# Block-sparse attention and SwiGLU: chunk 0's feed-forward part in float16, with the weights' low parts made on GpSimd

## The chip, the cores and the metric

The kernel runs on one core of one Trainium2 chip. The metric is the device time of one execution in microseconds (us), as the median of several runs. A core has five engines, each with an instruction queue of its own that it works through in order: TensorE (PE in the profile; its weight loads are PEld), VectorE (DVE), ScalarE (ACT), GpSimd (POOL) and SyncE (SP), which here only starts transfers. An instruction that waits for a semaphore holds up everything behind it on its engine.

## The reference

Four batches of eight heads attend over 768 positions of 64 numbers each. The mask lets a block of 32 rows see its neighbours, the first and the last block, and three sampled ones; the first and the last block see everything. The result, as x with 512 columns, goes through a SwiGLU feed-forward part with 1536 inner columns:

```python
scores = scale * np.matmul(q, k.transpose(0, 1, 3, 2))
scores = np.where(mask, scores, -1000000000.0)
attn = np.exp(scores - np.max(scores, axis=-1, keepdims=True))
attn = attn / (np.sum(attn, axis=-1, keepdims=True) + 1e-09)
attn_out = np.matmul(attn, v)
x = np.ascontiguousarray(attn_out.transpose(0, 2, 1, 3)).reshape(B * S, H * D)
g = x @ w_gate
silu = g * (1.0 / (1.0 + np.exp(-g)))
return (silu * (x @ w_val)) @ w_out
```

All inputs arrive as float64, seen by the kernel as pairs of int32.

## The kernel before, in words

The 3072 rows of x are worked on in eight **chunks**, two to a batch, of 384 rows each. A chunk first has its attention: query blocks (32 rows, 8 heads) in pairs, and in odd chunks the two blocks that see everything (`full_rows`). Names carry the block's number: `qk_13` are scores, `pv_13` products with the values, `p_5` a gate or value product of the feed-forward part, `po_0` an output product.

**Precision.** Nearly all matmuls take float16 operands in two parts: a high part (the rounded number) and a low part (what is left of it). Three products, high by high, high by low and low by high, are summed. Operands are first scaled by a power of two that comes from a norm: squares with their sum on ACT (`square_w`), a matmul with ones on PE (`norm`, `col_sums`), four small integer operations on DVE (`pow2`). `split_w` then makes the high part of a weight tile of 128x512 on ACT (`hi_part`, line 354) and the low part on DVE (`lo_part`, line 357). Both overwrite the float32 tile that stands one place ahead in the same memory, so tile f can be split only after tile f−1.

**Weights.** There are 36 such tiles: gate and value (w1raw, in memory `w_99` and `w_100`), and output (w2raw, in `w_101`), 12 of each. Each is loaded by one transfer and decoded from float64 to float32 by three DVE operations (`to_f32`, lines 382 to 384).

**Feed-forward part of a chunk** (`ffn`). For each of 12 inner tiles f: gate product and value product on PE (12 matmuls each, line 1369), tanh on ACT, two multiplications on DVE, the high part of h on ACT (1387) and its low part on POOL (1390). Then three output products `po_t` of 36 matmuls, each evacuated by ACT (1305). Chunk 0 is the exception: `ffn_first` multiplies the float32 x, which `x_keep` put aside, with the float32 weights (lines 1255 and 1291), so it needs neither norms nor splits. The weights' norms and splits come later, with ranks 14 and 16, during and after this part and before chunk 1's.

**Chunk 0's attention** also differs (`first`): the probabilities are turned by matmuls with a diagonal matrix that carries the softmax's reciprocals (`dg`, DVE line 1106; `turn_pe`; `turned_high` on ACT; `turned_low` on DVE, line 1128), not by transfers. Its keys are gathered into `kring` by POOL (lines 1002 to 1005), in later chunks by DVE. The values of every pair of blocks are gathered by a transfer that POOL starts (`vring`, line 1016).

**Order.** Nothing runs in the order of the source. Every piece of work is a task of a `Plan` with an engine, a duration in us, a rank and the buffers it takes from rings. `Plan.order` runs through time: whenever an engine is free, it takes the ready task of lowest rank whose buffers are free. The rank is moved by the table `SHIFT`, keyed by the piece of work. The durations therefore decide the order of each engine's queue, but at run time only semaphores hold it. `DMA_US` and `SEM_US` are the plan's times for a transfer's landing and a semaphore.

## Time and profile before

| Quantity | us |
|---|---|
| median of three runs | 847.31 |
| the three runs | 847.08, 849.96, 847.31 |
| profiled execution, its own time | 845.61 |
| its span in the profile | 843.8 |

The profile covers one execution. Its span is 1.8 us shorter than that execution's time, and that execution is 1.7 us below the median. The granted TensorE clock was 0.965 of full speed on average. Busy times overlap, so they don't add up to the span. A line of a group reads: line of the program, engine, operation, output<-inputs, shapes, count | busy us, mean ns of one | idle time of the engine ahead of it, and what ended that idle time. A line of the chain reads: start, duration, what. A line of an engine's timeline begins with start and duration too, and has in brackets how long the engine had been idle and what it waited for. A line of the windows has the stretch, its length and the busy us of PE, PEld, DVE, ACT and POOL with the number of instructions, then the granted clock, the share of transfers and GB/s.

### The profile page before, as it was taken

To read this page: it belongs to the slowest core of one execution; us is meant where nothing else is said; L and a number is where in the kernel's file an instruction comes from. 1 tells how busy PE (TensorE), PEld (TensorE's weight loads), DVE (VectorE), ACT (ScalarE), POOL (GpSimd) and SP (SyncE) were. 2 spreads that over 40 slices of the span, in tenths; PEclk is the share of its full clock that TensorE was granted. 3 is DMA by queue.
4 is the path that set the end of the run, shared out by engine and by line. 5 is a ranking of instruction groups with operands and counts; after the bars stand their busy time and mean duration, and the time that the engine had idled before them with its cause. 6 is when DMAs were issued, how large, how long until landed. Compare 5 with 4: busy or idle time off the path is not lost.

```text
span 843.8 us, 20625 instructions
## 1 busy us (share of the span) xinstructions
PE 769.2 (91%) x7634; PEld 460.9 (55%) x7634; DVE 592.1 (70%) x1784; ACT 528.4 (63%) x1266; POOL 200.7 (24%) x258
## 2 busy tenths in 40 slices
PE   0267799979999999999999999998999999999997
PEld 0246655545465655665566556663566556655653
DVE  5987989858888976896488757852679769821320
ACT  5855845669786766788467757873458658821220
POOL 5574100002014321231223211321123212310220
PEclk9757999989999999999999999999999999999999
DMA  9999785789947897899878876988847964820001
GB/s 292 256 280 274 213 241 164 146 200 185 220 128 220 186 228 138 191 180 232 218 179 180 182 167 132 199 173 243 210 96 143 193 145 103 169 57 26 1 1 38
DMA packets 196309, 144.05 MB, mean 171 GB/s; under 512 B 133104, under 2 KB 156272, under 8 KB 196208
## 3 DMA queue, kind: packets, MB, share of 16 engines
q1 hardware_dynamic: 190576, 125.42, 65.2%
q0 software_dynamic: 5632, 17.31, 8.3%
q8 instruction: 60, 0.98, 0.5%
q14 instruction: 41, 0.34, 0.1%
HBM read 86.58 MB, written 12.58 MB: 118 GB/s over the span
## 4 chain that ended last, share of the span: by engine, by line
PE 68%; DMA 15%; DVE 7%; ACT 3%; issue 3%; SPq 2%; POOL 1%; DVEq 0%; ACTq 0%; POOLq 0%
PE p L1369 33%; PE po L1416 13%; DMA pts<-pp 6%; PE pv L1168 6%; PE p L1255 5%; PE po L1291 4%; PE qk L1030 3%; DMA w<-vd 2%; DVE w L383 2%; DVE w L384 1%; PE pvf L875 1%; DMA qn<-in_q_dram 1%; DMA kraw<-in_k_dram 1%; PE qkf L806 1%; DMA qs<-qraw 1%
## 5 line engine op out<-in xcount | busy, mean ns | idle before, releaser
L1369 PE MATMUL p<-xt,w 128*128 128x384 f16 x2016 | 340.3, 326 | 0.0
L1369 PEld LDWEIGHTS <-w 128*128 128x128 f16 x2016 | 191.9, 98 | 128.4 <-issue 6.2
L1416 PE MATMUL po<-w,h 128*128 128x512 f16 x756 | 171.1, 381 | 0.0
L1390 POOL TENSOR_TENSOR h<-act,h 128x384 f16<-128x384 f32 x84 | 80.0, 953 | 304.4 <-ACT h L1387 304.1
L1016 POOL DMA_INDIRECT vring<-vd,vidx x82 | 78.6, 959 | 280.4 <-PE pv L1168 236.9
L1416 PEld LDWEIGHTS <-h 128*128 128x128 f16 x756 | 71.9, 98 | 87.2 <-issue 7.1
L1376 DVE SCALAR_TENSOR_TENSOR act<-act,p 128x384 f32<-128x384 f32 x84 | 46.1, 549 | 64.3 <-ACT act L1373 62.6
L1168 PEld LDWEIGHTS <-vring 128*128 128x128 f16 x1968 | 68.9, 99 | 28.2 <-issue 16.2
L357 DVE SCALAR_TENSOR_TENSOR pp<-e,rr,pp 128x256 f16<-128x256 f32 x152 | 77.7, 552 | 7.5 <-ACT pp L354 6.2
L1168 PE MATMUL pv<-pts,vring 128*128 128x64 f16 x1968 | 72.3, 194 | 11.0 <-DMA pts<-pp 6.3
L1373 ACT ACTIVATE act<-p,gsc 128x384 f32<-128x384 f32 x84 | 48.4, 577 | 52.8 <-PE p L1369 45.2
L1095 ACT ACTIVATE e<-e,nb,es 128x256 f32<-128x256 f32 x132 | 78.2, 593 | 2.2
L1387 ACT CAST h<-act 128x384 f16<-128x384 f32 x84 | 42.5, 505 | 54.4 <-DVE act L1379 53.9
L354 ACT ACTIVATE pp<-e,rr 128x256 f16<-128x256 f32 x152 | 67.8, 497 | 10.3 <-DMA ptsf<-ppf 3.6
L1255 PE MATMUL p<-xt,w 128*128 128x384 f32 x192 | 70.1, 520 | 1.3 <-ACT xt L1134 1.0
L1379 DVE SCALAR_TENSOR_TENSOR act<-act,hs,p 128x384 f32<-128x384 f32 x84 | 51.3, 611 | 22.9 <-PE p L1369 21.7
L1255 PEld LDWEIGHTS p<-xt,w 128*128 128x128 f32 x192 | 37.6, 202 | 27.6 <-issue 5.3
L1076 DVE CUSTOM_DVE_ANT_1 e<-qk,msk 128x256 f32<-128x256 f32 x132 | 50.0, 416 | 0.5 <-PE qk L1030 0.3
L1005 DVE COPY kring<-kst 128x256 f16 x228 | 46.0, 258 | 4.9 <-PE pv L1168 1.6
L1305 ACT ACTIVATE ot<-po,oc 128x512 f32<-128x512 f32 x21 | 14.4, 686 | 52.7 <-PE po L1416 52.2
L1194 DVE TENSOR_TENSOR xt<-pv,xt 64x256 f16<-64x256 f32 x76 | 31.9, 420 | 17.2 <-ACT xt L1189 14.1
L361 ACT ACTIVATE wsq<-w 128x512 bf16<-128x512 f32 x36 | 22.6, 628 | 25.6 <-DVE w L384 16.4
(168 smaller groups left out, 983.0 us busy)
## 6 DMA issues: line engine op xcount, KB each, us to landing
vring<-vd SPq DMA_DIRECT2D x82, 192.0 KB
w1raw<-in_w_dram SPq DMA_DIRECT2D x24, 512.0 KB
qs<-qraw SPq DMA_DIRECT2D x84, 128.0 KB
qn<-in_q_dram SPq DMA_DIRECT2D x48, 128.0 KB
w2raw<-in_w_dram SPq DMA_DIRECT2D x12, 512.0 KB
vfull<-vd SPq DMA_DIRECT2D x12, 512.0 KB
qraw<-in_q_dram SPq DMA_DIRECT2D x42, 128.0 KB
out_dram<-ot SPq DMA_DIRECT2D x20, 256.0 KB
```

The lines of the kernel that those rows point to most:

```text
L354: nc.scalar.activation(hi, src, AF.Copy, scale=scale)
L357: nc.vector.scalar_tensor_tensor(lo, src, scale, hi, op0=ALU.mult, op1=ALU.subtract)
L1016: nc.gpsimd.indirect_dma_start(vf[0:96, 1, :], None, bt.vd, bass.IndirectOffsetOnAxis(ap=vidx[0:96, qb : qb + 1], axis=0))
L1076: nc.vector.tensor_tensor_reduce(ev[:, g], stv[:, g], o.g.msk[:, qb, :].unsqueeze(2).broadcast_to([P, 8, BLK]), scale=1.0, scalar=-3.0e38, ...
L1095: nc.scalar.activation(ev[:, g], sv[:, g], AF.Exp, bias=nb_[:, g : g + 1], scale=o.g.es[:, 0:1], accum_out=c["rs"][:, g : g + 1],)
L1168: nc.tensor.matmul(pvv[:, j, n % 2], vg[:, cc, l, 2 * j : 2 * j + 2, :], pq[:, g, m, cc, u : u + 2, :], start=i == 0, stop=i == 5,)
L1255: nc.tensor.matmul(buf.tile[:, 0:T], wst[m][:, f + 1, k_ * P : (k_ + 1) * P], x_f32()[:, k_, :], start=k_ == 0, stop=k_ == NKT - 1,)
L1369: nc.tensor.matmul(t[:, 0:T], w_[:, f, m, k_, :], xt.tile[:, l, k_, :], start=i == 0, stop=i == 11)
L1373: nc.scalar.activation(get(act, f"act_{ci}_{f}"), pg.tile[:, 0:T], AF.Tanh, scale=c["gsc"][:, f : f + 1])
L1379: nc.vector.scalar_tensor_tensor(act.tile, act.tile, c["hs"][:, 1:2], pw.tile[:, 0:T], op0=ALU.mult, op1=ALU.mult)
L1390: nc.gpsimd.tensor_tensor(hv()[:, 1, :], act.tile, hv()[:, 0, :], op=ALU.subtract)
L1416: nc.tensor.matmul(po.tile, hv[:, l, ts_], wo16[:, f, m, :], start=f == 0 and i == 0, stop=f == NF - 1 and i == 2)
```

## The change

Chunk 0's feed-forward part now runs through `ffn(0)`, like the others': `ffn_first`, `x_keep` and `x_f32` are gone. The first-layer weights are scaled in three groups of inner tiles (0 and 1, 2 to 5, 6 to 11); a group's norm takes all its squares and those before it. `split_w` has three steps on two engines: POOL scales the float32 tile in place, ACT casts it to the high part, POOL subtracts that to get the low part. The diagonals of chunk 0 are made by ACT. The two edge key blocks of chunk 0 are copied by one DVE operation, not by two of POOL. All durations of the plan, the ranks of the splits and the whole of `SHIFT` are new.

```diff
-W1_DEC, W2_DEC, W1_SPLIT, W2_SPLIT = 3.0, 5.0, 14.0, 16.0
+W1_DEC, W2_DEC, W1_SPLIT, W2_SPLIT = 3.0, 5.0, 3.05, 5.5
+W1_GROUPS = ((0, 2), (2, 6), (6, 12))
-DMA_US = 2.0
-SEM_US = 0.1
+DMA_US = 2.2
+SEM_US = 0.16
 SHIFT = {
-    "a0.0": -105.32, "a0.1": 0.02, "a0.2": -38.31, "a1.0": -72.7, "a1.1": -11.99, "a1.2": -2.34, "a2.0": -13.58, "a2.1":
+    "a0.0": -202.11, "a0.1": 56.45, "a0.2": -35.15, "a1.0": -198.18, "a1.1": -93.69, "a1.2": -28.19, "a2.0": -10.14,
...
-    t_rep = add("POOL", 8.0, repeats, [t_tab], rank=TAB)
+    t_rep = add("POOL", 17.0, repeats, [t_tab], rank=TAB)
...
     def split_w(m, f, scale, rank, need, last):
         src, hi, lo = wst[m][:, f + 1, :], w16[m][:, f, 0, :], w16[m][:, f, 1, :]
-        before = w_read[m][f - 1] if f else []
-        t1 = add("ACT", 0.72, lambda: hi_part(hi, src, scale), need + before + [last], rank)
-        return add("DVE", 0.75, lambda: lo_part(lo, src, scale, hi), [t1], rank)
+        before = v_first[RING] if m == 2 and f == 0 else []
+        t0 = add("POOL", 0.85, lambda: nc.gpsimd.tensor_scalar(src, src, scale, None, op0=ALU.mult), need, rank)
+        t1 = add("ACT", 0.6, lambda: nc.scalar.copy(hi, src), before + [t0, last], rank)
+        return add("POOL", 1.2, lambda: nc.gpsimd.tensor_tensor(lo, src, hi, op=ALU.subtract), [t1], rank)
...
     def split_w1(rank):
         last = [None, None]
-        for f2 in range(0, NF, 2):
+        for f0, f1 in W1_GROUPS:
+            fs, k = slice(f0, f1), f1 - f0
...
+            t = add("PE", 0.08, norm, sq + [x[0] for x in w1_split[-1:]], rank + 0.1 * f0, take=[n])
+            t = add("DVE", 0.75, scale, [t], EVAC, use=[n])
...
+        def edges():
+            two = bt.ks.tile.rearrange("p h (s k) -> p h s k", k=BLK)
+            nc.vector.tensor_copy(kg[:, :, 3:8:4, :], two[:, :, 0 : NB : NB - 1, :])
...
-            if first:
-                d = get(dg, f"dg_{nq}").bitcast(F32).rearrange("p (g q) -> p g q", g=4)
-                for g in range(2):
-                    nc.vector.tensor_scalar(d[:, g], ident, c["rr"][:, g : g + 1], None, op0=ALU.mult)
+        def diagonal():
+            d = get(dg, f"dg_{nq}").bitcast(F32).rearrange("p (g q) -> p g q", g=4)
+            for g in range(2):
+                nc.scalar.activation(d[:, g], ident, AF.Copy, scale=c["rr"][:, g : g + 1])
...
+        gated = {}
+        for f0, f1 in W1_GROUPS if ci == 0 else ((0, NF),):
+            t = add("DVE", 0.15, lambda fs=slice(f0, f1): gate_scale(fs), [w1_split[f1 - 1][0], batches[b].vsc_t], EVAC)
...
     decode_w1(W1_DEC)
+    split_w1(W1_SPLIT)
     decode_w2(W2_DEC)
-    ffn_first(1000.0)
+    split_w2(W2_SPLIT)
+    ffn(0, 1000.0)
...
-        if ci == 1:
-            split_w1(W1_SPLIT)
-            split_w2(W2_SPLIT)
```

Three places of the queues show what the new order does. The first is **PE** in the middle of chunk 0's gate and value products (`p_5` and its neighbours; `nrm_w` is the norm of a group of weights). Before:

```order
L1255 MATMUL p_5_2006<-xt_124,w_99 128x384 x4
L1255 MATMUL p_5_2022<-xt_124,w_100 128x384 x4
L1255 MATMUL p_6_2040<-xt_124,w_99 128x384 x4
L1255 MATMUL p_6_2061<-xt_124,w_100 128x384 x2
L351 LDWEIGHTS ones_h
L351 MATMUL nrm_w_2_2068<-wacc,ones_h 128x4
L1255 MATMUL p_6_2061<-xt_124,w_100 128x384 x2
```

and now:

```order
L1314 LDWEIGHTS w_99
L1314 MATMUL p_5_2136<-xt_125,w_99 128x384
L355 LDWEIGHTS ones_h
L355 MATMUL nrm_w_6_2159<-wacc,ones_h 128x12
L1314 LDWEIGHTS w_100
L1314 MATMUL p_5_2161<-xt_125,w_100 128x384
```

The last group's norm, which needs the squares of all tiles 6 to 11, stands between the gate and the value product of tile 5; before, a norm of two tiles stood there and no product needed it.

The second is **POOL** behind the last key copies and gathers of chunk 0. Before, it has only gathers of values and then the low parts of chunk 1's h:

```order
L1016 DMA vring_113<-vd_115,vidx 96x1024
L1016 DMA vring_114<-vd_115,vidx 96x1024
L1016 DMA vring_112<-vd_115,vidx 96x1024
L1390 TENSOR_TENSOR h_0_3539<-act_0_3517,h_0_3539 128x384
L1390 TENSOR_TENSOR h_0_3539<-act_1_3567,h_0_3539 128x384
L1390 TENSOR_TENSOR h_2_3715<-act_2_3660,h_2_3715 128x384
```

and now, where the last group's scale has come (w0 and w1 are the gate and value tiles):

```order
L1335 TENSOR_TENSOR h_0_4_2157<-act_0_4_2112,h_0_4_2157 128x384
L422 TENSOR_SCALAR w0_99<-w0_99,wsc_102 128x512
L422 TENSOR_SCALAR w1_100<-w1_100,wsc_102 128x512
L422 TENSOR_SCALAR w0_99<-w0_99,wsc_102 128x512
L422 TENSOR_SCALAR w1_100<-w1_100,wsc_102 128x512
L1335 TENSOR_TENSOR h_0_4_2157<-act_0_5_2174,h_0_4_2157 128x384
L422 TENSOR_SCALAR w0_99<-w0_99,wsc_102 128x512
L422 TENSOR_SCALAR w1_100<-w1_100,wsc_102 128x512
L422 TENSOR_SCALAR w0_99<-w0_99,wsc_102 128x512
L424 TENSOR_TENSOR w0_99<-w0_99 128x512
L424 TENSOR_TENSOR w1_100<-w1_100 128x512
```

Seven scalings and one low part of h now stand ahead of the first subtraction of the last group, which ends the split of tile 6.

The third is **DVE** at the last first-layer weight that it decodes (w1raw_6_1, tile 6's value weights), now:

```order
L1321 SCALAR_TENSOR_TENSOR act_0_4_2112<-act_0_4_2112,p_0_4_2088 128x384
L386 TENSOR_SCALAR w1_100<-w1raw_6_1_2049 128x512
L387 SCALAR_TENSOR_TENSOR w1_100<-w1raw_6_1_2049,w1_100 128x512
L388 SCALAR_TENSOR_TENSOR w1_100<-w1raw_6_1_2049,w1_100 128x512
L1324 SCALAR_TENSOR_TENSOR act_0_4_2112<-act_0_4_2112,hs_0_1967,p_0_4_2114 128x384
L386 TENSOR_SCALAR w2_101<-w2raw_3_2076 128x512
L387 SCALAR_TENSOR_TENSOR w2_101<-w2raw_3_2076,w2_101 128x512
L388 SCALAR_TENSOR_TENSOR w2_101<-w2raw_3_2076,w2_101 128x512
L346 TENSOR_SCALAR p2_w1_6_2177<-nrm_w1_6_2159 128x12
```

One more output weight is decoded between that weight and the powers of two of the last group; the split of tiles 6 to 11 waits for these.

244 lines of the change are left out of this document (92 added, 152 removed), and 97 rows, old and new, of the table SHIFT.

## The prediction, made before the result was known

> **What bounds the kernel now.** I read the busy shares and the chain of waits first, then the stretch around chunk 0's feed-forward part.
>
> ```profile
> PE 769.2 (91%) x7634; PEld 460.9 (55%) x7634; DVE 592.1 (70%) x1784; ACT 528.4 (63%) x1266; POOL 200.7 (24%) x258
> PE 68%; DMA 15%; DVE 7%; ACT 3%; issue 3%; SPq 2%; POOL 1%; DVEq 0%; ACTq 0%; POOLq 0%
> ```
>
> TensorE (PE) is busy for 91% of the span and carries 68% of the chain. Where are the other 9%? The windows give busy time of PE, weight loads, DVE, ACT and POOL in each stretch (then granted clock and DMA share).
>
> ```profile
> 84.00:105.00 21.00, 15.46 (x295) 13.04 (x294) 19.83 (x48) 17.00 (x45) 4.09 (x4) 0.92 0.76 212
> 105.00:126.00 21.00, 21.00 (x66) 11.83 (x65) 17.45 (x35) 9.64 (x25) 0.00 (x0) 0.92 0.84 244
> 168.00:189.00 21.00, 14.91 (x187) 9.13 (x188) 11.78 (x40) 12.04 (x35) 1.83 (x2) 0.84 0.83 190
> 231.00:843.00 612.00, 599.93 (x5828) 353.55 (x5826) 400.67 (x1287) 374.74 (x896) 142.32 (x150) 1.00 0.70 151
> ```
>
> From 231 us on PE idles 12 us in 612. So the change's worth is settled by when chunk 1's feed-forward part starts; I call that point T1. All of chunk 1's attention stands ahead of T1 on PE in both orders, so what T1 moves, the end moves. POOL does nothing at all from 105 to 126 us.
>
> The chain shows each kind of matmul alone, then PE's own rows the two ends and the waits:
>
> ```profile
> 102.46 10.93 PE p L1255 x24
> 155.06 4.07 PE p L1255 x12
> 189.59 1.29 PE p L1255 x4
> 203.26 5.25 PE po L1291 x12
> 769.48 46.80 PE p L1369 x288
> 816.28 23.32 PE po L1416 x108
> ```
> ```profile
> 172.07 0.27 PE L1051 MATMUL qk<-kst,qs 128*32 128x96 f16 x8 [3.29 <-ACT e L1095]
> 183.79 0.91 PE L1168 MATMUL pv<-pts,vring 128*128 128x64 f16 x14 [2.60 <-DMA pts<-pp]
> 221.78 0.81 PE L1337 MATMUL xn<-sqx,ones_h 128*128 128x384 bf16 x4
> 231.12 6.01 PE L1369 MATMUL p<-xt,w 128*128 128x384 f16 x36
> ```
>
> T1 is 231.1 before. Chunk 0's gate and value products run from 102.5 to 190.9 (88.4 us), its output products from there to T1 (40.2 us).
>
> **What the matmuls give.** Float32 gate and value: 192 records of 4.07/12 = 0.339 us, 65.1 us; a whole float16 chunk is 46.8. That is 18.3 less. Output: 72 of 5.25/12 = 0.4375 us, 31.5, against 23.3: 8.2 less. Chunk 0 now needs the x norm too, four matmuls, some 0.7. So 25.8 us less on PE. Of the 88.4 us, 65.1 are those matmuls at full clock, 2.7 more the slow clock of the first 24 (10.93 against 24 × 0.339 = 8.2), some 6 the two idle times shown; the remaining 14.5 are chunk 1's attention, the same list in both orders. PE alone would need 46.8 + 14.5 + 0.7 = 62 us from p_0 to the end of p_11, then 40.2 − 8.2 = 32 to T1. By PE alone T1 would be 102.5 + 62 + 32 = 196.5, 35 earlier. But float32 products need no scaled weights; the float16 ones do, and that work now stands ahead of them.
>
> **What now comes first.** The split costs, per weight tile of 128x512, one POOL scaling, one ACT cast and one POOL subtraction; 36 tiles. On POOL only these rows come near:
>
> ```profile
> L1390 POOL TENSOR_TENSOR h<-act,h 128x384 f16<-128x384 f32 x84 | 80.0, 953 | 304.4 <-ACT h L1387 304.1
> L329 POOL TENSOR_SCALAR dup<-dup 128x192 f32<-128x192 f32 x1 | 0.7, 695 | 0.1
> L316 POOL TENSOR_SCALAR df<-df 128x24 f32<-128x24 f32 x3 | 0.9, 284 | 0.3
> L1005 POOL COPY kring<-kst 128x256 f16 x36 | 17.5, 524 | 13.4 <-PE qk L1051 10.9 <-issue 2.5
> ```
>
> The subtraction is the low part of h, 4/3 as long: 0.953 × 512/384 = 1.27 at most, 1.22 if the fixed part does not grow; I take 1.22. The scaling has no near row. Its upper end is the slope of the two TENSOR_SCALARs, 0.695 + 320 × 0.411/168 = 1.48; its lower end is the bare copy, at 256 columns, not doubled: 0.52. I take 0.9, nearer to a doubled copy (1.05) than to the slope, since the copy's mean is stretched by waits.
>
> **Start of p_0.** DVE loses 24 diagonals; ACT gains them, and group 1's casts and squares:
>
> ```profile
> L1106 DVE TENSOR_SCALAR dg<-ident,rr 128x128 f32<-128x128 f32 x24 | 6.4, 324 | 0.4
> L1090 ACT ACTIVATE nb<-mx,es 128x2 f32<-128x2 f32 x88 | 25.4, 289 | 17.8 <-DVE mx L1076 9.1 <-DVE mx L1069 8.2
> L1387 ACT CAST h<-act 128x384 f16<-128x384 f32 x84 | 42.5, 505 | 54.4 <-DVE act L1379 53.9
> L361 ACT ACTIVATE wsq<-w 128x512 bf16<-128x512 f32 x36 | 22.6, 628 | 25.6 <-DVE w L384 16.4 <-issue 8.2 <-DVE rs L648 0.5
> ```
>
> A 128x128 one on ACT lies between 0.289 and 0.505; by columns 0.36, so 24 are 8.7 us. In 84 to 105 us ACT has 4.0 idle, DVE 1.2. A gain of 2 to a loss of 6: I take 3 lost, p_0 at 105.5.
>
> **The third group.** Gate tiles 6 to 11 wait for the scale of all twelve, that for the last first-layer weight decoded on DVE.
>
> ```profile
> 99.85 0.68 DVE L1128 TENSOR_TENSOR pts<-pt,pts 128x512 f16<-128x512 f32 x1
> 141.41 0.69 DVE L384 SCALAR_TENSOR_TENSOR w<-w1raw,w 128x512 int32<-128x512 int32 x1
> L382 DVE TENSOR_SCALAR w<-w1raw 128x512 int32<-128x512 int32 x24 | 10.4, 434 | 4.2 <-DMA w1raw<-in_w_dram 4.2
> L383 DVE SCALAR_TENSOR_TENSOR w<-w1raw,w 128x512 int32<-128x512 int32 x24 | 16.9, 703 | 0.8
> L384 DVE SCALAR_TENSOR_TENSOR w<-w1raw,w 128x512 int32<-128x512 int32 x24 | 17.0, 707 | 0.8
> L1376 DVE SCALAR_TENSOR_TENSOR act<-act,p 128x384 f32<-128x384 f32 x84 | 46.1, 549 | 64.3 <-ACT act L1373 62.6 <-ACT pp L354 1.2
> L1379 DVE SCALAR_TENSOR_TENSOR act<-act,hs,p 128x384 f32<-128x384 f32 x84 | 51.3, 611 | 22.9 <-PE p L1369 21.7
> ```
>
> The last turned low part of chunk 0 ends at 100.5, the last decode at 142.1. The new DVE list has between the two ten decodes (10 × 1.84 = 18.4), nine products near 0.58 (5.2) and some twenty reductions, norms and small scalings (about 5.8): 29.4, their small overlaps left in. With the 3 us from above: 103.5 + 29.4 = 132.9. POOL now works beside it (below), for which I add 5: 138. The square (0.63 and its sum), the norm and the powers of two take about 2.5: the scale is there at 140.5. PE, which needs some 25 us to the end of p_5, has been waiting since about 131.
>
> POOL then has, ahead of gate tile 6's second low part, 7 scalings, a low part of h and 2 subtractions: 6.3 + 0.95 + 2.44 = 9.7. p_6 starts at 150.2. From there to what p_11 waits for POOL has 17 scalings, 16 subtractions, 4 low parts of h and a gather: 15.3 + 19.5 + 3.8 + 1.0 = 39.6, where PE has 37. POOL paces this, and I add 4 for its waits: 193.8. With 32 us for the output, T1 = 225.8, 5.3 earlier. The profiled execution took 1.8 us more than its span, 845.6; 5.3 less is 840.3; the median of the three runs is 1.7 above the profiled one: **842**.
>
> Costed at nothing: the two edge copies moved to DVE as one (0.3 us, DVE gained 6 from the diagonals), the gathers behind POOL's new work (chunk 1's values are read only in p_9 and later; six 0.96 us gathers, worth up to 5 if PE reaches them first), and the changed order after T1, where 12 us of idle are all there is to win.
>
> **The price of sharing.** How much DVE and POOL hold each other up decides the sign, so here are a pair of DVE low parts beside POOL and one alone:
>
> ```profile
> 273.05 2.23 DVE L357 SCALAR_TENSOR_TENSOR pp<-e,rr,pp 128x256 f16<-128x256 f32 x2
> 279.25 0.87 DVE L357 SCALAR_TENSOR_TENSOR pp<-e,rr,pp 128x256 f16<-128x256 f32 x2
> ```
> ```profile
> 272.50 1.15 POOL L1016 DMA_INDIRECT vring<-vd,vidx  x1 [2.71 <-PE pv L1168]
> 273.67 0.93 POOL L1390 TENSOR_TENSOR h<-act,h 128x384 f16<-128x384 f32 x1
> ```
>
> The pair lost 1.36 of the 1.55 us in which POOL was busy behind its start. DVE's operations with two inputs in SBUF are, in the segment up to the last decode, 20 × 0.70 = 14; under POOL's lead some 7.5; in p_6 to p_11 some 12 (two decodes, probability low parts). Together 33.5 us that can at worst be added to the path; none is the other end. My 9 (5 + 4) is a quarter, because in the first segment POOL has only 20 us of work in 30, and later DVE is not the pacer. This trace agrees with a rule of the Trainium skill, page "SBUF — State Buffer", section "Who interferes with whom": a DVE instruction with two SBUF inputs and a GpSimd one that reads SBUF share a port pair, and whichever starts first blocks the other entirely. By that rule taken in full the sum would end at T1 = 250, and the change would be slower; it speaks against putting this work on GpSimd while DVE decodes.
>
> **Rivals.** *Port lock (slower).* POOL's back-to-back runs hold DVE's decodes, so the third scale is late, and later DVE's two-input work holds POOL. Without waits my T1 is 216.8; every us of waits adds one, so from 14.3 us of them the change loses. Two thirds of 33.5, 22, give T1 = 239 and 855; all give 866. For it: the pair above. Against: h's low parts on POOL have a mean of 953, near the undisturbed 0.93, beside a DVE busy 65% of the time.
>
> *ACT takes over (no change).* ACT's rows for its new and old work there, and a stretch in which it is full:
>
> ```profile
> L354 ACT ACTIVATE w<-w,wsc 128x512 f16<-128x512 f32 x24 | 16.5, 714 | 1.2 <-DVE w L357 0.7 <-PE p L1255 0.5
> L1095 ACT ACTIVATE e<-e,nb,es 128x256 f32<-128x256 f32 x132 | 78.2, 593 | 2.2
> L354 ACT ACTIVATE pp<-e,rr 128x256 f16<-128x256 f32 x152 | 67.8, 497 | 10.3 <-DMA ptsf<-ppf 3.6 <-issue 1.5 <-ACT pp L354 1.1
> L1373 ACT ACTIVATE act<-p,gsc 128x384 f32<-128x384 f32 x84 | 48.4, 577 | 52.8 <-PE p L1369 45.2 <-POOL h L1390 4.1 <-DVE oc L1350 2.4
> 189.00:210.00 21.00, 21.00 (x282) 11.77 (x271) 17.85 (x61) 20.55 (x52) 4.18 (x5) 1.00 0.95 188
> ```
>
> From the third scale to h's part of tile 11 ACT has 21 casts of weights (15.0), 12 exponents with their sums and 12 probability parts (15.4), 7 tanh and 8 casts of h (8.1), 7 squares (5.7) and the full rows and small ones (some 14): 58 us by single durations. Consecutive records overlap: the full stretch's 52 last 24.2 added up by their groups and 20.55 as busy time. So 58 are about 49, level with POOL's 9.7 + 39.6. As the casts sit between POOL's two steps, the two queues wait on each other: 140.5 + 49 and 10 us of such waits, less 1 that lies behind p_11, and 32 give T1 = 230.5 and 847. For it: two in-order queues of one length; against: POOL has scalings to do while a cast is late.
>
> *PE-bound (much faster).* Scaling at 0.52, no waits, p_0 unmoved: last decode 129.9, lead 7, p_6 at 139.4, then PE's 37 and 32: T1 about 208, 824. Nothing shows POOL that quick.
>
> **How the numbers follow.** 842 has 0.43, port lock 0.28, ACT 0.17, PE-bound 0.12. Less than 0.5% (4.2 us, about what this kernel's measurement can tell) is no change. From 842 come 0.33 faster, 0.09 same, 0.01 slower; from the lock 0.03 same, 0.25 slower; from ACT 0.02, 0.12, 0.03; PE-bound is all faster: together 0.47, 0.24 and 0.29. The forecast's own range is 832 to 849 (waits of none to 16). The whole one is 822 to 862: it reaches PE-bound below and most of the full lock above.
>
> **What would show it.** Right: PE idle of 15 to 25 us ahead of p_6, released by POOL's subtraction; scaling near 0.9, subtraction near 1.22; gate and value matmuls 0.16 us apiece; DVE decodes under 0.8 each; T1 near 226. Wrong: L387 and L388 well above 0.8, or POOL subtractions above 1.5 (lock); PE released by ACT's cast (ACT); no wait at p_6 (PE-bound); a start of p_0 past 110, or idle after T1 other than 12 us, which none of the cases holds.

## The result, and the profile after

The changed kernel takes 876.0 us (median of four runs, 867.4 to 883.8) against 848.6 for the kernel before: 1.028 times as long, with a 95% interval of 1.023 to 1.034. Ratios leave out executions in a slower state of the chip, here the one of 883.8 us; the other three have a median of 872.5. The forecast was 842, with a range of 822 to 862. The sign was wrong.

The page of the changed kernel, busy shares and then the chain's shares by engine:

```profile
PE 759.2 (87%) x7767; PEld 456.3 (52%) x7767; DVE 600.0 (69%) x1724; ACT 534.6 (61%) x1303; POOL 314.0 (36%) x336
PE 62%; DVE 15%; POOL 7%; DMA 6%; issue 5%; ACT 4%; SPq 1%; DVEq 0%; POOLq 0%; ACTq 0%
```

PE's busy time fell by 10 us where the sum had 26. In the chain its share fell from 68% to 62%, while DVE's rose from 7% to 15% and POOL's from 1% to 7%. The windows (busy us of PE, PEld, DVE, ACT, POOL) show where:

```profile
105.00:126.00 21.00, 14.05 (x126) 9.16 (x124) 20.13 (x32) 7.95 (x16) 18.95 (x13) 0.83 0.65 191
147.00:168.00 21.00, 6.77 (x22) 2.69 (x22) 20.03 (x32) 7.90 (x19) 17.22 (x12) 0.58 0.45 137
189.00:210.00 21.00, 11.51 (x277) 7.69 (x277) 17.55 (x43) 13.88 (x40) 21.00 (x17) 0.64 0.73 153
```

Before, PE was busy for 21.00 of 21 us in each of these. Now DVE is nearly full in the first two and POOL is full in the third, and PE is full in none. PE's own timeline gives the points of the forecast's sum: p_0, the third group's norm, p_6 (begun, then stopped for its value weights), the first output product and T1.

```profile
110.05 0.32 PE L1314 MATMUL p<-xt,w 128*128 128x384 f16 x1
149.22 0.17 PE L355 MATMUL nrm_w<-wacc,ones_h 128*128 128x12 bf16 x1 [5.39 <-ACT wsq L365]
161.80 0.82 PE L1314 MATMUL p<-xt,w 128*128 128x384 f16 x2 [8.56 <-ACT w L423]
166.08 8.07 PE L1314 MATMUL p<-xt,w 128*128 128x384 f16 x34 [3.46 <-POOL w L424]
223.41 2.11 PE L1361 MATMUL po<-w,h 128*128 128x512 f16 x9
261.12 4.06 PE L1314 MATMUL p<-xt,w 128*128 128x384 f16 x24
```

T1 is 261.1: 30 us later than before (231.1), and 35 later than forecast (225.8). Behind T1 there were 612.7 us before and are 609.6 now, so nearly the whole loss lies ahead of T1. POOL's new groups:

```profile
L424 POOL TENSOR_TENSOR w<-w 128x512 f16<-128x512 f32 x36 | 45.1, 1266 | 18.1 <-ACT w L423 17.9
L422 POOL TENSOR_SCALAR w<-w,wsc 128x512 f32<-128x512 f32 x24 | 40.5, 1700 | 1.3 <-DVE wsc L350 1.1
L422 POOL TENSOR_SCALAR w<-w,oss 128x512 f32<-128x512 f32 x12 | 19.2, 1614 | 0.1
```

The subtraction takes 1.27 us, the upper end of its bounds. The scaling takes 1.61 to 1.70, above even the upper bound of 1.48, and not 0.9. Beside them DVE's decodes of the output weights, first in the kernel before, then in the changed one:

```profile
L383 DVE SCALAR_TENSOR_TENSOR w<-w2raw,w 128x512 int32<-128x512 int32 x12 | 8.3, 693 | 0.4
L384 DVE SCALAR_TENSOR_TENSOR w<-w2raw,w 128x512 int32<-128x512 int32 x12 | 8.3, 692 | 0.4
L382 DVE TENSOR_SCALAR w<-w2raw 128x512 int32<-128x512 int32 x12 | 5.0, 418 | 0.0
```
```profile
L387 DVE SCALAR_TENSOR_TENSOR w<-w2raw,w 128x512 int32<-128x512 int32 x12 | 12.2, 1013 | 0.4
L388 DVE SCALAR_TENSOR_TENSOR w<-w2raw,w 128x512 int32<-128x512 int32 x12 | 12.0, 999 | 0.4
L386 DVE TENSOR_SCALAR w<-w2raw 128x512 int32<-128x512 int32 x12 | 8.7, 727 | 0.0
```

The same instructions on the same data became 44% to 74% longer. DVE doesn't count as waiting in them; it counts as busy. Two rows of each timeline show one case, DVE first, POOL after it:

```profile
112.66 1.97 DVE L388 SCALAR_TENSOR_TENSOR w<-w2raw,w 128x512 int32<-128x512 int32 x1
114.55 1.38 DVE L386 TENSOR_SCALAR w<-w2raw 128x512 int32<-128x512 int32 x1
```
```profile
108.75 5.30 POOL L422 TENSOR_SCALAR w<-w,wsc 128x512 f32<-128x512 f32 x3
114.03 2.91 POOL L424 TENSOR_TENSOR w<-w 128x512 f16<-128x512 f32 x2
```

The last scaling ends at 114.05; the decode that began at 112.66 ends at 114.6. The next one, of one input, begins at 114.55 under the first of the two subtractions and ends at 115.9, a full us before the second one does. So a run of POOL's operations does not stop DVE for its whole length. The run of four scalings ahead of p_6 shows it, DVE first, POOL after it:

```profile
156.10 0.69 DVE L386 TENSOR_SCALAR w<-w2raw 128x512 int32<-128x512 int32 x1
156.83 1.05 DVE L387 SCALAR_TENSOR_TENSOR w<-w2raw,w 128x512 int32<-128x512 int32 x1
157.92 0.69 DVE L388 SCALAR_TENSOR_TENSOR w<-w2raw,w 128x512 int32<-128x512 int32 x1
```
```profile
151.85 6.37 POOL L422 TENSOR_SCALAR w<-w,wsc 128x512 f32<-128x512 f32 x4 [1.14 <-DVE wsc L350]
```

Between 84 us and T1, the two-input decodes that ran beside scalings alone have a mean of 0.99 us, those beside subtractions alone 1.20, and those with POOL idle 0.69 (11, 5 and 9 of them). Summed over the records of DVE in that stretch, its operations lasted some 40 us longer than the shortest of their form; in the kernel before it was about 3.

### The profile page after: what moved, and what is told of

The parts are those of the page before. It is cut to its first block, busy times and chain, and to the rows that moved or that the text cites. A ratio compares the mean times of both kernels' runs of the same rounds, so it can differ in the third digit from the quotient of the medians.

```text
span 870.7 us, 20969 instructions
## 1 busy us (share of the span) xinstructions
PE 759.2 (87%) x7767; PEld 456.3 (52%) x7767; DVE 600.0 (69%) x1724; ACT 534.6 (61%) x1303; POOL 314.0 (36%) x336
## 4 chain that ended last, share of the span: by engine, by line
PE 62%; DVE 15%; POOL 7%; DMA 6%; issue 5%; ACT 4%; SPq 1%; DVEq 0%; POOLq 0%; ACTq 0%
PE p L1314 34%; PE po L1361 15%; PE pv L1167 5%; POOL w L422 4%; PE qk L1037 3%; DMA kraw<-in_k_dram 2%; DMA pts<-pp 2%; DVE w L387 2%; DVE w L388 2%; POOL w L424 2%; DVE pp L361 1%; DVE w L386 1%; PE qk L1058 1%; PE qkf L813 1%; ACT e L1102 1%
## 5 line engine op out<-in xcount | busy, mean ns | idle before, releaser
L1314 PE MATMUL p<-xt,w 128*128 128x384 f16 x2304 | 397.9, 331 | 16.1 <-ACT w L423 8.6
L1314 PEld LDWEIGHTS <-w 128*128 128x128 f16 x2304 | 221.6, 99 | 179.9 <-issue 23.8
L1335 POOL TENSOR_TENSOR h<-act,h 128x384 f16<-128x384 f32 x96 | 93.5, 975 | 326.7 <-ACT h L1332 322.3
L1361 PE MATMUL po<-w,h 128*128 128x512 f16 x864 | 197.3, 379 | 0.1
L1023 POOL DMA_INDIRECT vring<-vd,vidx x82 | 77.8, 949 | 150.9 <-PE pv L1167 127.7
L1361 PEld LDWEIGHTS <-h 128*128 128x128 f16 x864 | 80.7, 98 | 91.3 <-issue 3.1
L1321 DVE SCALAR_TENSOR_TENSOR act<-act,p 128x384 f32<-128x384 f32 x96 | 52.7, 549 | 62.1 <-ACT act L1318 61.4
L1324 DVE SCALAR_TENSOR_TENSOR act<-act,hs,p 128x384 f32<-128x384 f32 x96 | 58.4, 609 | 19.2 <-PE p L1314 17.0
L1188 ACT CAST xt<-pv 64x256 f16<-64x256 f32 x88 | 32.1, 364 | 41.6 <-PE pv L1167 39.4
L424 POOL TENSOR_TENSOR w<-w 128x512 f16<-128x512 f32 x36 | 45.1, 1266 | 18.1 <-ACT w L423 17.9
L1097 ACT ACTIVATE nb<-mx,es 128x2 f32<-128x2 f32 x88 | 25.5, 290 | 27.1 <-DVE mx L1083 25.2
```

Source lines behind the costliest of these rows:

```text
L424: return add("POOL", 1.2, lambda: nc.gpsimd.tensor_tensor(lo, src, hi, op=ALU.subtract), [t1], rank)
L1023: nc.gpsimd.indirect_dma_start(vf[0:96, 1, :], None, bt.vd, bass.IndirectOffsetOnAxis(ap=vidx[0:96, qb : qb + 1], axis=0))
L1314: nc.tensor.matmul(t[:, 0:T], w_[:, f, m, k_, :], xt.tile[:, l, k_, :], start=i == 0, stop=i == 11)
L1321: nc.vector.scalar_tensor_tensor(act.tile, act.tile, 1.0, pg.tile[:, 0:T], op0=ALU.add, op1=ALU.mult)
L1324: nc.vector.scalar_tensor_tensor(act.tile, act.tile, c["hs"][:, 1:2], pw.tile[:, 0:T], op0=ALU.mult, op1=ALU.mult)
L1335: nc.gpsimd.tensor_tensor(hv()[:, 1, :], act.tile, hv()[:, 0, :], op=ALU.subtract)
```

## The experiments

All start from the changed kernel, except the last one, which stands behind the table. Ratios are to the kernel before, run on the same chip beside them. "Third norm" is the point at which PE has the norm of tiles 6 to 11, that is, all first-layer weights decoded and squared. These points come from one profiled execution of each kernel. "Beside" means that POOL does its work and nothing uses the result.

| Kernel | time us | ratio, 95% interval | p_0 | third norm | po_0 | T1 |
|---|---|---|---|---|---|---|
| changed | 876.0 | 1.028, 1.023 to 1.034 | 110.1 | 149.2 | 223.4 | 261.1 |
| no scaling | 856.3 | 1.010, 1.007 to 1.014 | 107.4 | 141.8 | 206.0 | 238.8 |
| POOL empty, two casts on ACT | 849.0 | 0.999, 0.996 to 1.003 | 102.2 | 131.3 | 191.1 | 227.4 |
| split on ACT and DVE | 856.8 | 1.007, 1.003 to 1.011 | 107.7 | 142.2 | 208.3 | 241.8 |
| diagonals on DVE | 878.3 | 1.036, 1.030 to 1.043 | 111.5 | 151.1 | 226.3 | 257.4 |
| low parts free | 844.2 | 0.991, 0.987 to 0.995 | 101.6 | 131.4 | 189.9 | 222.9 |
| POOL beside | 871.2 | 1.023, 1.013 to 1.032 | 106.0 | 144.0 | 210.0 | 254.1 |
| scaling with two inputs | 887.2 | 1.043, 1.034 to 1.051 | 108.1 | 152.6 | 230.9 | 265.2 |
| split on DVE, gate and value weights first | 856.1 | 1.006, 1.002 to 1.010 | 105.4 | 139.9 | 204.1 | 238.4 |
| low parts free, less decoding | 836.6 | 0.981, 0.977 to 0.985 | 104.1 | 132.9 | 185.7 | 217.6 |
| memsets beside, longer | 892.6 | 1.043, 1.037 to 1.049 | 105.3 | 145.3 | 227.5 | 270.9 |
| memsets beside, as long | 861.9 | 1.012, 1.006 to 1.017 | 107.1 | 141.2 | 208.2 | 248.9 |
| POOL beside, no low part of h | 864.8 | 1.016, 1.011 to 1.021 | 108.2 | 143.5 | 209.5 | 246.2 |
| memsets beside, no low part of h | 855.6 | 1.006, 1.002 to 1.010 | 107.6 | 135.9 | 191.5 | 236.5 |

### What POOL's work costs, and what the rest would be worth

**Without the scaling.** The split's first step is empty.

```diff
-        t0 = add("POOL", 0.85, lambda: nc.gpsimd.tensor_scalar(src, src, scale, None, op0=ALU.mult), need, rank)
+        t0 = add("POOL", 0.85, lambda: None, need, rank)
```

> The changed kernel with POOL's 36 scalings left out (the weights are split unscaled, so the output is wrong); the order of everything else is kept. Theory PRICE (the loss is that a scaling takes 1.65 us on POOL, not the 0.9 of the forecast): the wait ahead of p_6 falls from 14 to about 3 us after the last scale, p_6 to p_11 from 57 to about 40, T1 from 261 to about 233, the time from 876 to about 848. Theory LOCK (POOL's work blocks DVE's decodes): with 20 us of POOL's work gone from the decode stretch it shrinks from 41 to about 33 us as well, T1 about 225, the time about 840. If neither holds, T1 stays above 250.

Measured: 856.3, T1 238.8. Of the 2.8% lost 1.8 are back, but neither forecast was met: the decodes came earlier, as LOCK has it (third norm 149.2 to 141.8), while p_6 to po_0 stayed at 52.5 us (57.3 in the changed kernel). Taking 17 scalings, 28 us of POOL, out of that stretch gave 5. So POOL's throughput did not pace it alone.

**POOL empty.** There is no scaling, and the subtraction is a second cast on ACT.

```diff
-        t0 = add("POOL", 0.85, lambda: nc.gpsimd.tensor_scalar(src, src, scale, None, op0=ALU.mult), need, rank)
+        t0 = add("POOL", 0.85, lambda: None, need, rank)
...
-        return add("POOL", 1.2, lambda: nc.gpsimd.tensor_tensor(lo, src, hi, op=ALU.subtract), [t1], rank)
+        return add("POOL", 1.2, lambda: nc.scalar.copy(lo, src), [t1], rank)
```

> The changed kernel with neither scaling nor subtraction on POOL; the low part is a second ACT cast of the unscaled tile (so the output is wrong). LOCK: decodes with both inputs in SBUF go back to 0.70 us, the stretch from the last turned low part to the last decode falls from 41 to about 30 us, T1 to about 215 to 220, the time to 830 to 835. PRICE alone, without lock: the stretch stays near 41, T1 about 233 as without the scaling, the time about 848. ACT has 36 more casts of 0.62, 22 us in all; if ACT paces, p_6 to p_11 stays above 45 us.

Measured: 849.0, T1 227.4. All the loss is back, and no gain appears. The third norm is at 131.3, 18 us ahead of the changed kernel, on a DVE list that is the same: PRICE alone does not do that. But T1 is 7 us later than the upper end of LOCK's figure (220).

**The split as before the change**, in the new order.

```diff
-        t0 = add("POOL", 0.85, lambda: nc.gpsimd.tensor_scalar(src, src, scale, None, op0=ALU.mult), need, rank)
-        t1 = add("ACT", 0.6, lambda: nc.scalar.copy(hi, src), before + [t0, last], rank)
-        return add("POOL", 1.2, lambda: nc.gpsimd.tensor_tensor(lo, src, hi, op=ALU.subtract), [t1], rank)
+        t0 = add("POOL", 0.85, lambda: None, need, rank)
+        t1 = add("ACT", 0.6, lambda: hi_part(hi, src, scale), before + [t0, last], rank)
+        return add("POOL", 1.2, lambda: lo_part(lo, src, scale, hi), [t1], rank)
```

> The changed kernel with the weights split as before: ACT makes the scaled high part, DVE the low part in one operation; POOL has none of it, and the result is right. PRICE: the wait ahead of p_6 is 3 us, p_6 to p_11 about 42, T1 about 229 to 235, the time about 845 to 850. LOCK: DVE takes 8 low parts of 0.74 in the decode stretch (6 us) but is blocked no more: stretch about 35, T1 about 228, time about 843. Rival, DVE too full: the stretch stays at 41 or grows and T1 stays above 240 (time above 855).

Measured: 856.8, T1 241.8: in time and T1 the third one, DVE too full, though the stretch to the last decode took 36.4 us, near LOCK's 35. DVE's windows from 126 us on (DVE has the third busy time) show how full it is:

```profile
126.00:147.00 21.00, 12.88 (x61) 6.59 (x61) 20.45 (x40) 11.12 (x26) 3.14 (x4) 0.84 0.55 173
147.00:168.00 21.00, 13.64 (x71) 7.05 (x72) 20.49 (x38) 13.11 (x29) 1.97 (x2) 0.76 0.67 184
```

The split with DVE's 36 operations in place of POOL's 72 is faster than the changed kernel, with a ratio of 1.007 against 1.028.

**Diagonals on DVE again.**

```diff
-                nc.scalar.activation(d[:, g], ident, AF.Copy, scale=c["rr"][:, g : g + 1])
+                nc.vector.tensor_scalar(d[:, g], ident, c["rr"][:, g : g + 1], None, op0=ALU.mult)
```

> The changed kernel with chunk 0's 24 diagonals on DVE again, at the same places of the order. Theory START (the diagonals on ACT make p_0 late, 110 for 102.5): p_0 starts 3 to 6 us earlier and the time falls to about 871. Rival (DVE paces chunk 0's attention, so ACT is the better place): p_0 starts 4 to 8 us later, the time is about 881.

Measured: p_0 at 111.5, 1.5 later, and 878.3. Theory START falls: the diagonals are not what made p_0 late. The rival's 4 to 8 us were too much, and the time is level with the changed kernel's.

**Low parts left out.**

```diff
-        return add("POOL", 1.2, lambda: nc.gpsimd.tensor_tensor(lo, src, hi, op=ALU.subtract), [t1], rank)
+        return add("POOL", 1.2, lambda: None, [t1], rank)
...
-                        nc.tensor.matmul(t[:, 0:T], w_[:, f, m, k_, :], xt.tile[:, l, k_, :], start=i == 0, stop=i == 11)
+                        nc.tensor.matmul(t[:, 0:T], w_[:, f, 0, k_, :], xt.tile[:, l, k_, :], start=i == 0, stop=i == 11)
```

(The output products likewise, and no scaling.)

> The changed kernel with neither scaling nor low parts of the weights at all: ACT casts the high part alone and the matmuls read it in place of the low part (so the output is wrong, the number of matmuls is the same). It shows what float16 in chunk 0 is worth when the split is nearly free. Theory ACT (in the run with POOL empty the 36 extra casts kept ACT full, 20.4 to 20.8 of 21 us, and PE waited for its exponents): T1 falls from 227 to about 217, the time to about 839. Theory DVE (decodes, products and chunk 1's attention on DVE set the pace whatever the split costs): T1 stays at 224 to 228 and the time at 846 to 850.

Measured: 844.2, T1 222.9. This is the whole worth of float16 in chunk 0 when the split costs one cast: 0.9%, 8 us of T1 out of PE's 26. T1 is nearer to theory DVE. PE's rows and DVE's windows:

```profile
131.35 0.17 PE L355 MATMUL nrm_w<-wacc,ones_h 128*128 128x12 bf16 x1 [4.42 <-ACT wsq L365]
141.57 8.88 PE L1314 MATMUL p<-xt,w 128*128 128x384 f16 x36 [6.19 <-ACT w L423]
```
```profile
126.00:147.00 21.00, 10.39 (x37) 4.65 (x36) 19.84 (x40) 10.75 (x28) 3.33 (x3) 0.60 0.58 168
147.00:168.00 21.00, 17.39 (x256) 10.67 (x255) 20.17 (x60) 18.61 (x46) 3.21 (x3) 0.99 0.73 170
```

PE is through with p_5 and waits for squares and casts of weights that DVE has just decoded. Its own work is not as short as the sum had it either. The granted clock is 0.60 in the first of these windows, and p_6's 36 matmuls behind the wait take 8.88 us, 0.25 each. Chunk 0's gate and value products are busy for 55.4 us here and 58.2 in the changed kernel; the sum had 46.8.

### Port or queue

**POOL beside.** From low parts free; POOL again does 36 operations of one and 36 of two inputs, on a constant.

```diff
+    def beside(op, scale=None):
+        to = w16[0][:, 0, 1, :].rearrange("p (a b) -> p a b", a=4)
+        ones = ident.unsqueeze(1).to_broadcast([P, 4, P])
+        if scale is not None:
+            nc.gpsimd.tensor_scalar(to, ones, scale, None, op0=op)
+        else:
+            nc.gpsimd.tensor_tensor(to, ones, to, op=op)
...
+        t0 = add("POOL", 0.85, lambda: beside(ALU.mult, scale), need, rank)
...
+        return add("POOL", 1.2, lambda: beside(ALU.subtract), [t1], rank)
```

> As the kernel with free low parts, but POOL again runs 36 scalings and 36 subtractions of 128x512 at their places, on a constant and into a place that nothing reads: nobody waits for them but the low parts of h behind them on POOL (so the output is wrong in the same way). LOCK: the DVE decodes are as slow as in the changed kernel (mean 0.85 to 1.0 for the two-input ones), the stretch to the last decode is 8 to 12 us longer than with free low parts and T1 10 to 20 us later. PRICE (only waiting for POOL's results cost time): decodes stay at 0.70 and T1 moves by less than 3 us.

Measured: 871.2, T1 254.1, 31 us later than with low parts free, more than LOCK had. PRICE falls as the main cause: of the 3.7% between low parts free (0.991) and the changed kernel (1.028), 3.2 come from POOL working. The 0.5 that are left for anyone's waiting for scalings and subtractions are less than the intervals. POOL's groups and the decodes:

```profile
L424 POOL TENSOR_TENSOR w<-ident,w 128x512 f16<-128x512 f32 x36 | 46.2, 1285 | 2.2
L422 POOL TENSOR_SCALAR w<-ident,wsc 128x512 f16<-128x512 f32 x24 | 40.8, 1700 | 3.1 <-DVE wsc L350 1.2
```
```profile
L388 DVE SCALAR_TENSOR_TENSOR w<-w2raw,w 128x512 int32<-128x512 int32 x12 | 11.3, 938 | 0.4
L387 DVE SCALAR_TENSOR_TENSOR w<-w2raw,w 128x512 int32<-128x512 int32 x12 | 10.2, 854 | 0.4
L386 DVE TENSOR_SCALAR w<-w2raw 128x512 int32<-128x512 int32 x12 | 8.9, 738 | 0.0
```

**A cheaper scaling.** In the changed kernel, as a product of two inputs.

```diff
-        t0 = add("POOL", 0.85, lambda: nc.gpsimd.tensor_scalar(src, src, scale, None, op0=ALU.mult), need, rank)
+        t0 = add("POOL", 0.85, lambda: nc.gpsimd.tensor_tensor(src, src, scale.to_broadcast([P, DO]), op=ALU.mult), need, rank)
```

> The changed kernel with POOL's scaling as a two-input product with the scale repeated along the row, in place of the one-input operation with a scale per partition. PRICE of the one-input form (1.65 us against 1.2 for a two-input one): a scaling takes about 1.2, POOL loses some 14 us, T1 falls by 6 to 9, the time to about 868. Rival (two inputs cost POOL as much, or two-input operations hold DVE longer): 874 to 878.

Measured: a scaling takes 1.12 instead of 1.67, POOL has 20 us less to do, and the kernel is slower: 887.2, a ratio of 1.043 against 1.028, above what the rival had. The timelines of DVE, then POOL, show what befell DVE:

```profile
106.23 6.89 DVE L443 SCALAR_TENSOR_TENSOR igv<-wsc 128x4 f32<-128x4 f32 x1
113.91 4.37 DVE L1289 TENSOR_SCALAR gsc<-wsc,vs 128x4 f32<-128x4 f32 x1
```
```profile
105.92 0.92 POOL L1023 DMA_INDIRECT vring<-vd,vidx  x1 [0.69 <-PE pv L1167]
106.86 3.03 POOL L422 TENSOR_TENSOR w<-w,wsc 128x512 f32<-128x512 f32 x3
109.85 2.25 POOL L424 TENSOR_TENSOR w<-w 128x512 f16<-128x512 f32 x2
112.07 1.03 POOL L422 TENSOR_TENSOR w<-w,wsc 128x512 f32<-128x512 f32 x1
113.25 0.94 POOL L1023 DMA_INDIRECT vring<-vd,vidx  x1 [0.16 <-issue]
114.22 4.03 POOL L422 TENSOR_TENSOR w<-w,wsc 128x512 f32<-128x512 f32 x4
```

A DVE operation on four columns, 0.17 us in the changed kernel, stands for 6.89 us: it ends when POOL's unbroken run of six operations does, at 113.1. The next small one is held for 4.37 by a run of four. Both began while POOL was starting a gather (L1023) just ahead of the run. So did the other holds through two or more whole operations of POOL: two more in this trace, one in the changed kernel (3.65 us, at 217.4) and one with POOL beside (2.47). Why is open. How much of the loss the holds make was not taken apart: T1 is 4 us later than in the changed kernel, and what stands behind T1 is 6 us longer (615.2 against 609.6).

**Memsets of POOL beside**, four for a scaling, three for a subtraction.

```diff
-        ones = ident.unsqueeze(1).to_broadcast([P, 4, P])
-        if scale is not None:
-            nc.gpsimd.tensor_scalar(to, ones, scale, None, op0=op)
-        else:
-            nc.gpsimd.tensor_tensor(to, ones, to, op=op)
+        for _ in range(4 if scale is not None else 3):
+            nc.gpsimd.memset(to, 0.0)
```

> As the run in which POOL works beside the path, but with memsets of 128x512 float16 in place of its scalings (four each) and subtractions (three each): POOL is busy at the same places and reads nothing from SBUF (the output is wrong as there). If DVE is held by POOL's reads of SBUF: the two-input decodes go back to about 0.70 to 0.75, T1 falls from 254 to about 225 to 230, the time to about 846. If any work of POOL holds DVE: decodes stay at 0.82 to 0.94 and the time above 860.

Measured: the two-input decodes are back at 0.71 to 0.74, as for reads. But the time is 892.6. The run changed two things, since its memsets (252 of 0.54, 136 us) make POOL's queue longer than the 107 us beside. So POOL's reads hold DVE, and a second cost hangs on the length of POOL's queue. It was repeated at equal length:

```diff
-        for _ in range(4 if scale is not None else 3):
+        for _ in range(3 if scale is not None else 2):
             nc.gpsimd.memset(to, 0.0)
+        if scale is None:
+            nc.gpsimd.memset(to[:, 0, :], 0.0)
```

> As the run with POOL beside the path, with memsets that last as long: three for a scaling (1.62 us by the 0.54 of one), two and a short one for a subtraction (about 1.28), so POOL's queue is as long as there and only its reads of SBUF are gone (the output is wrong as there). READS hold DVE: two-input decodes at 0.70 to 0.75, the third group's norm near 133 (131.4 with POOL empty, 144.0 beside), T1 near 235 to 243, since what stands behind on POOL (gathers, low parts of h) is late as there; time 853 to 862. QUEUE alone (what stands behind on POOL is late, the port does not matter): the norm still comes early, but T1 and time are as beside, 254 and 871. ANY activity of POOL holds DVE: norm at 144, time 871.

Measured: 861.9, third norm 141.2, T1 248.9, and decodes of 0.70 to 0.74: none of the three as a whole. The waits of ACT in this run, with total, times and longest, name what stands in the queue:

```profile
ACT act L1325 <- POOL h L1342: 21.6, 4, 7.6
ACT act L1325 <- PE p L1321: 6.1, 4, 3.3
```

The low part of h is POOL's, behind its new work. Until it is made, one of the two buffers for tanh's result is taken, and tanh on ACT waits: 21.6 us.

**Without chunk 0's low parts of h**, once beside, once with memsets.

```diff
-                nc.gpsimd.tensor_tensor(hv()[:, 1, :], act.tile, hv()[:, 0, :], op=ALU.subtract)
+                if ci:
+                    nc.gpsimd.tensor_tensor(hv()[:, 1, :], act.tile, hv()[:, 0, :], op=ALU.subtract)
...
-                            po.tile, hv[:, l, ts_], wo16[:, f, 0, :], start=f == 0 and i == 0, stop=f == NF - 1 and i == 2
+                            po.tile, hv[:, l if ci else 0, ts_], wo16[:, f, 0, :], start=f == 0 and i == 0, stop=f == NF - 1 and i == 2
```

> As the run with POOL beside the path, and chunk 0's 12 low parts of h are left out too: the output products read the high part twice (so the output is wrong). Nothing but the gathers of values waits for POOL any more. If DVE held by POOL's reads is the larger part of the 31 us of T1 that POOL's work costs: T1 stays at 244 or more (254 beside, 223 with POOL empty), the time at 862 or more. If the low parts of h behind POOL's long queue are the larger part: T1 falls below 240, the time below 858.

> The same with memsets in place of scalings and subtractions: neither reads of SBUF nor low parts of h, only the gathers behind POOL's queue and whatever a mere write of POOL holds up. If those two are all: the third group's norm at 131 to 135, T1 at 225 to 231 (a gather of 6 us among it), the time at 846 to 850. If T1 stays above 240, the queue costs time in a way that is not named yet.

Measured: 864.8 with T1 246.2, its first forecast, and 855.6 with T1 236.5, between its two. In the second the two-input decodes are at 0.69 to 0.70 and po_0 is at 191.5, level with low parts free (189.9): with neither reads nor low parts of h, the gate and value products lose nothing. What is left is one wait between po_0 and T1:

```profile
PE pv L1174 <- DMA vring<-vd,vidx: 10.8, 1, 10.8
```

That is a gather of chunk 1's values, which POOL starts behind its new work. So T1 goes from 222.9 (low parts free) to 236.5 with the gathers late, to 246.2 with POOL's reads as well, and to 254.1 with the low parts of h late too. As ratios: 0.991, 1.006, 1.016, 1.023. The costs are not free to add in another order: with memsets, the low parts of h cost 12 us of T1 (248.9 against 236.5), with reads 8. And they hide one another: with reads po_0 is 18 us later than with memsets (209.5 against 191.5), and the wait for the gather behind it falls from 10.8 to 1.1. In the changed kernel neither of the two waits above stands. There the same queue shows as waits for the split: from 100 us to T1 ACT's casts wait 14.6 us for POOL's scalings and subtractions, and PE's gate and value products 6.9 for subtractions.

### What paces DVE's side

**Gate and value weights first**, in the kernel with the split on DVE: four ranks in `SHIFT`.

```diff
-    4.77, "d2.0": 580.68, "d2.1": 45.24, "d2.10": -237.67, "d2.11": -29.24, "d2.2": -421.9, "d2.3": 29.65, "d2.4": 40.98,
-    "d2.5": 34.49, "d2.6": -516.85, "d2.7": 37.7, "d2.8": -157.98, "d2.9": 90.1, "f1": 260.77, "f1.0": 39.72, "f1.1":
+    4.77, "d2.0": 580.68, "d2.1": 45.24, "d2.10": 0, "d2.11": -29.24, "d2.2": 0, "d2.3": 29.65, "d2.4": 40.98,
+    "d2.5": 34.49, "d2.6": 0, "d2.7": 37.7, "d2.8": 0, "d2.9": 90.1, "f1": 260.77, "f1.0": 39.72, "f1.1":
```

> The kernel with the split on ACT and DVE as before the change, and four output-weight decodes that stood among the last first-layer ones moved behind them (four numbers of the table that sets the ranks). Theory THIRD GROUP (tile 6 waits for the last first-layer decode): that decode ends 5 to 8 us earlier, p_6 too, T1 about 236, the time about 851. Theory DVE (its whole list sets T1): p_6 is earlier, the later products give it back, T1 stays within 2 us of 242 and the time at 855 to 858.

Measured: third norm 2.2 us earlier, T1 3.4, time 856.1 against 856.8. For the norm that is less than half of what theory THIRD GROUP had, for T1 a little more than half, and p_0 is 2.3 earlier as well. The time did not move: nearer to theory DVE.

**Less decoding**, from low parts free; `one` is set for the output weights alone.

```diff
         nc.vector.tensor_scalar(d, hi, 5, 2, op0=ALU.logical_shift_left, op1=ALU.logical_shift_right)
+        if one:
+            return
```

> The kernel with free low parts, and of the three decode operations of the 12 output weights only the first is run (so the output is wrong): 12 times 1.4, 17 us less on DVE, four of those decodes ahead of the last first-layer one. Theory DVE (DVE's list, full to 20 of 21 us from 84 to 168 us, sets the pace once the split is free): the third group's norm falls from 131.4 to about 125, T1 from 223 to about 210 to 214, the time from 844 to about 833. Rival (from there PE and its waits for ACT set the pace): T1 falls by less than 4 us, the time stays above 840.

Measured: 836.6, T1 217.6. DVE carries part of it: 17 us less on DVE are 8 us less of time (0.981 against 0.991). But T1 fell by 5.3, between the two forecasts, and the third norm did not come earlier (132.9, 131.4 before). DVE is no longer full there; it works through its list in order, and in it stand products that wait for ACT's tanh (3.5 us from 100 to 135). DVE's windows here:

```profile
105.00:126.00 21.00, 20.43 (x128) 11.88 (x128) 15.88 (x34) 15.59 (x36) 3.21 (x3) 1.00 0.74 220
126.00:147.00 21.00, 13.66 (x65) 7.15 (x64) 16.67 (x39) 13.11 (x34) 3.15 (x3) 0.84 0.71 207
```

**The kernel before with diagonals on ACT**, the one part that loads neither DVE nor POOL.

```diff
-                    nc.vector.tensor_scalar(d[:, g], ident, c["rr"][:, g : g + 1], None, op0=ALU.mult)
+                    nc.scalar.activation(d[:, g], ident, AF.Copy, scale=c["rr"][:, g : g + 1])
```

> The kernel before, with only chunk 0's diagonals moved to ACT, at the same places. DVE loses 24 operations of 0.32 and ACT gains 24 of 0.39. If DVE paces chunk 0's attention: p_0 starts 2 to 5 us earlier than 102.5 and the time is 2 to 5 us under the kernel before. If PE's products or ACT do: no change, within 2 us.

Measured: 848.9, ratio 0.996, 0.993 to 1.000. p_0 did not come earlier (103.8), T1 neither (233.5): by these points the second forecast. The time is 0.4% lower, between 0 and 0.7, which would fit the first one as well; the profiled execution does not show where it comes from.

No kernel here that does all the work clearly beats the kernel before. The new order of the plan alone, in the kernel before, was not tried.

## Why the prediction was wrong

**What held.** That T1 settles the time: behind it lie 612.7 us before, 609.6 after, and 610 to 620 in the other runs. That p_6 would be the place of the stall, behind the third scale; but PE waited there 8.6 us for ACT's cast and 3.5 for POOL's subtraction, where the forecast had 15 to 25 ended by the subtraction. That the subtraction costs about 1.22 (1.27). That DVE's list from the last turned low part to the last decode has some 29.4 us: it takes 30 with memsets and no low parts of h, and 31.5 with low parts free.

**Where the 35 us are.** T1 came 35 us after the forecast's. The last turned low part was 4 late. The stretch of decodes took 40.9 for 34.4, from there to the third scale 3.5 for 2.5, POOL's lead to p_6 14.2 for 9.7, p_6 to po_0 57.3 for 43.6, and from po_0 to T1 37.7 for 32.

**The step that failed first is the price of sharing.** It was bounded from none to 33.5 us and taken as 9, a quarter, "because in the first segment POOL has only 20 us of work in 30, and later DVE is not the pacer". POOL's reads alone, against memsets as long, move po_0 by 18 us (no low parts of h in either): 7 in the stretch of decodes (30 to 37.2) and 9 between p_6 and po_0 (46.6 to 55.4) are the largest parts. In the changed kernel the stretch of decodes is 11.5 over the list's 29.4, where 5 was taken; POOL had 31 us of work in it, not 20. What was missed is that DVE had no slack to absorb it. Its windows of the kernel before, two of which the prediction shows, had 17.5 to 20.1 of 21 from 84 to 168 us; these are the other two:

```profile
126.00:147.00 21.00, 20.78 (x71) 11.62 (x70) 20.14 (x50) 10.46 (x26) 0.00 (x0) 1.00 0.56 162
147.00:168.00 21.00, 21.00 (x259) 12.37 (x259) 19.65 (x54) 14.56 (x36) 0.00 (x0) 1.00 0.76 153
```

The rival of the port lock was right in sign and place, and its full value (T1 250, 866) was still too low. It counted the lock alone. At T1 the reads alone show as 5 to 10 us (248.9 to 254.1, and 236.5 to 246.2), since a part of their price is hidden under other waits. The 31 us that POOL's work beside costs at T1 hold what stands behind its queue too. How the 35 us of the changed kernel divide between the two is not shown.

**The scaling was mis-sized**: 0.9 taken, 1.61 to 1.70 measured, above the bound of 1.48. Seven of them ahead of p_6 are 5 us and seventeen in p_6 to p_11 some 12 more than forecast: nearly what these two steps were late (4.5 and 13.7). But the run without scaling shows that this sum is not the cause by itself: the stretch from p_6 to po_0 then still took 52.5 us where 43.6 were forecast. POOL's long operations cost less here by being waited for than by what they held up.

**What waits behind POOL's queue** was put at nothing in the sum, and at up to 5 us for the gathers. With memsets of equal length and no low parts of h T1 was 13.6 us late, 10.8 of it one wait for a gather. The low parts of h, which were in the sum only as POOL's time, cost 8 to 12 more, because tanh has two buffers. Both prices are those of kernels in which nothing waits for the split.

**The gain was over-stated.** By PE alone T1 was to be 35 us earlier at best, and the PE-bound rival had 23 (T1 208). With a nearly free split it is 8. One step that failed is "What bounds the kernel now": PE at 21.00 of 21 was read as the bound, but DVE beside it was at 17.5 to 20.1, and the float32 products need only decoded weights, while the float16 ones need all of a group decoded and squared. Shorter matmuls then turn into waits on DVE's list. That DVE carries this is shown only in part: taking 17 us from DVE gave 8 of time. The other is a term of the sum: chunk 0's gate and value matmuls were to take 0.16 us apiece, 46.8 in all. They took 0.20, 58.2 in all, and 55.4 with low parts free, because those behind a wait were slow: 8.07 us for 34 of p_6, with a granted clock of 0.58 from 147 to 168 us, against 4.06 for 24 at T1.

**The start of p_0** was 110.1, not 105.5, and past the 110 that none of the cases held. The diagonals are not the reason. With POOL empty p_0 is at 102 to 104, with work of POOL beside at 105 to 108, but with the split on DVE and none of it on POOL at 107.7 and 105.4 too. What makes it late was not told apart. By itself it need not cost anything: with memsets and no low parts of h p_0 is at 107.6 and po_0 still at 191.5.

**ACT** did not bound the changed kernel. Where it got more to do it did: with POOL empty and 36 more casts, ACT was at 20.4 to 20.8 of 21 from 147 us on and T1 4.5 us later than without them.

The profile's signs were named rightly: decodes "well above 0.8" were the mark of the lock, and they are there (1.0). The rule of the Trainium skill, page "SBUF — State Buffer", section "Who interferes with whom", speaks of two inputs in SBUF against a GpSimd instruction that reads SBUF, with one side blocked entirely. The runs agree: two-input decodes of 0.85 to 0.94 with POOL reading, 0.70 to 0.74 with memsets as long, and 0.69 to 0.70 when the low parts of h, which read too, are gone. By that rule in full the forecast would have been on the right side. The same section of the Trainium skill says that VectorE in one of its 2-port modes contends with GpSimd, and does not limit this to reads. The one-input decode takes 0.42 alone and 0.55 beside memsets, which fits it; in which mode it ran no trace here shows.

## What to carry to other kernels

Work that is moved to GpSimd is not free beside a full VectorE. Here it cost more than doing it on VectorE (a ratio of 1.028 against 1.007), and most of that remained when nobody waited for its results (1.023). Before such a move, look at how full VectorE is in that stretch and how much of GpSimd's new work reads its operands while VectorE runs: in the changed kernel VectorE's operations lasted some 40 us longer beside 124 us of GpSimd's. Then list what stands behind in GpSimd's queue, gathers above all, with the buffers that they keep. And where one engine is at 100%, look at the second: here it was at 83% to 96%, and a cut that the sum put at 26 us on the first was worth 8.

## What the hardware showed that was not expected

- A one-input scaling of 128x512 float32 with a scale per partition takes 1.56 us on GpSimd at its shortest, longer than a two-input product of the same size (1.03) or the subtraction (1.14).
- VectorE can be held for a whole unbroken run of GpSimd's operations, 6.89 us for one of 0.17. Most holds in the changed kernel end with the operation that runs. Those through two or more whole operations, here and in two of the runs, began while GpSimd was starting a gather. VectorE is counted as busy meanwhile.
- A shorter operation on GpSimd can be the worse neighbour: with the two-input scaling POOL's total fell by 20 us, and the kernel went from a ratio of 1.028 to 1.043.
